# Banded attention and a two-layer MLP on one core: the order table of all five engines replaced by that of another search

## The chip, the core and the metric

The kernel runs on one core of a Trainium2 chip. The metric is the device time of one execution in microseconds (us), the median of the runs given. The core's engines each take their instructions strictly in order: PE (TensorE, matrix products), DVE (VectorE), ACT (ScalarE), POOL (GpSimd) and SP (SyncE, which here only issues DMA transfers). What one engine needs of another it waits for at a semaphore, and everything queued behind the waiting instruction waits too.

## The reference

```python
def _attn_ref(q_l, k_l, v_l, q_g, k_g, v_g):          # 8 batches, 8 heads, 512 local + 32 global, D = 64
    k_all = np.concatenate([k_g, k_l], axis=2); v_all = np.concatenate([v_g, v_l], axis=2)
    out_g = np.matmul(sm(scale * np.matmul(q_g, k_all.transpose(0, 1, 3, 2))), v_all)
    s_ll = np.where(np.abs(pos[:, None] - pos[None, :]) <= 32, scale * q_l @ k_l.T, -1e9)
    s_l = np.concatenate([scale * q_l @ k_g.T, s_ll], axis=-1)
    out_l = np.matmul(sm(s_l), v_all)                 # sm: softmax over the last axis
    return np.concatenate([out_g, out_l], axis=2)
def _moe_ref(x, w_in, w_out):                         # x 4352 x 512, w_in 512 x 2048, w_out 2048 x 512
    h = x @ w_in
    return (h * np.cos(h)) @ w_out
reference = _moe_ref(_attn_ref(...).transpose(0, 2, 1, 3).reshape(B * S, H * D), w_in, w_out)
```

## The kernel before

All products run in fp16 planes: a value is split into a high and a low part, and a product is three PE products (high by high, high by low, low by high). Batch 0 and the scores of batch 1 run in fp32 while the weights are still being decoded.

**Attention** goes by pairs of heads (`b, p`: batch and pair). Of a pair, `load_qk` fetches q and k, `qk_a` to `qk_c` find a scale (`qk_b` is one small PE product, `pm_qk`), `qk_d` splits: ACT writes the high part `qa` (line 916), DVE the low part `kl` (line 917). `qk_e` moves halves of them between partitions by three SP steps, the first from `qa` (lines 928, 929), the second from `kl` once the first has landed (line 931), the third after the second (line 933). Then `sc_a` makes the scores of one of four windows on PE (`ps`, lines 1184 and 1185, the first against `kh`, the second against `kl`), `sc_b` adds the mask on DVE, `sc_c` takes the exponential on ACT, `sc_d` normalizes on POOL (line 1230), casts to the high plane on ACT (line 1235) and subtracts for the low plane on POOL (line 1237), both planes in `plx`. `sc_e` transposes a window's planes by one SP transfer into `ptb` (line 1242), and `av_a` multiplies them with v on PE (`acc`, line 1274). Of a batch, `v_q`, `v_b` and `v_c` find v's scale (`v_b` is the PE product `pm_v`, line 855).

**The MLP** goes by chunks of 256 tokens, 17 of them (the last holds the global rows), each in eight blocks of 256 hidden columns: `m1_a` (24 products `ph` on PE, line 1432), `m1_b` to `m1_d` (cosine and product on ACT and DVE, split into `gh` on ACT, line 1478, and `gl` on POOL, line 1479), `m2_a` (products `po`, lines 1585 to 1587). From chunk 4 on, the first two blocks of a chunk take seven smaller products in place of eight (`sv_a`, `sv_y`, line 1530). PE interleaves the MLP of one batch with the attention of the next.

**The weights** (`w_in_load`, `w_in_max`, `w_in_piece`, and the same for `w_out`) are loaded as 64-bit integers, searched for their maximum and decoded on DVE, ACT and POOL during the first part of the program.

What sets the order: `body` records every step's instructions, and then reads `ORDER`, one string per engine. A word such as `23.4x3` names step 23, its instruction 4 of that engine, and three in a row; each instruction named gets a dependency on the one named before it, so that the string is the engine's queue:

```python
        for name, line in ORDER.items():
            mine = [[i for i in step if i.engine == getattr(E_, name)] for step in steps]
            at_, prev, used = defaultdict(int), None, set()
            for word in line.split():
                word, _, times = word.partition("x")
                k, _, i = word.partition(".")
                at_[k] = int(i or at_[k])
                for _ in range(int(times or 1)):
                    ins = mine[int(k)][at_[k]]
                    at_[k] += 1
                    if prev is not None:
                        tc.add_manual_dep(ins, prev.name, order, reason="order")
                    prev = ins
```

On ACT the exponential and the cosine need different function tables; a table load (`ACT_TABLE_LOAD`) is put in wherever the order changes from the one to the other.

Of the kernel before, what the change touches and what calls it, by code (L numbers as in the profile page):

```python
# [22 lines left out]
        18x4 22x4 23.4 23.0 23.5 23.1x2 23.6 23.3 23.7 27x4 29.4x3 29.0 29.7 29.1x3 33 33.2 33.1 33.3 35  # L23
        35.4 35.1x3 35.5x3 28x8 34x8 40 40.4 40.1 40.5 40.2 40.6x2 40.3 57 49 69x4 39x8 41x8 74 74.2
        74.1 74.3 64x24 67x24 72x24 108 108.2 108.1 108.3 91x24 106x24 125x24 109 109.4 109.1 109.5
        109.2 109.6 109.3 109.7 135x24 110x2 110.4 110.2 110.5x2 110.3 110.7 124 112x8 113x8 127 127.2
        127.1 127.3 141 141.4x4 141.1x3 143x24 149x8 150 150.4 150.1 150.5 150.2 150.6 150.3 150.7 164x3
        155x5 151x8 152x8 156x20 157x8 164 189x5 164x19 189x3 170x3 170.4 170.3 164 176x22 171x2 189x4
        176x2 187x2 171x18 195x4 196 196.2 196.1 196.3 187x22 206x24 208.6 208.0 208.7 208.1x2 208.8x2
        208.3 208.10 208.4 208.11 208.5 204 209x4 210 210.2 210.1 210.3 227x24 229x2 229.6x2 229.2 229.8  # L30
        229.3x3 229.9x3 250 250.6x3 250.1x2 250.9x2 250.3x3 250.11 274 274.6 274.1x3 274.7x2 274.4 274.9
        274.5 274.10x2 288.6 288.0 288.7 288.1x3 288.8x4 288.4x2 230x18 231x3 231.4x4 231.3 233 233.2
        233.1 233.3 300x2 300.6x3 300.2x2 300.9 300.4x2 300.10 248x24 272x21 234 234.2 234.1 234.3
        230x18 300 303.6 303.0x3 303.7x3 303.3x3 303.10x2 251x2 252x4 272x3 311x12 251x2 253x4 251x32
        313.6 313.0x5 313.7x3 313.5 313.10x2 318x2 318.6x2 318.2x4 318.8x4 286x24 275x13 276x8 325
        325.6x2 325.1 325.8x3 325.2x3 325.11 325.5 329.6 329.0 329.7 275x23 289 290 349x4 329.1x5
        329.8x4 294x60 333x2 333.6x2 333.2x4 333.8x4 289x35 349x5 371x5 307x30 319 322 307x30 381x5
        349x15 371x19 326 330 339.6 339.0x3 339.7x2 339.3 339.9x2 326x3 330x3 339.4x2 339.11 335x4 340x4
        351x3 351.6 351.3x3 351.7x5 381x19 356x4 357x8 358 395x24 373x4 374x8 410x24 384x4 397x5 424x24
        436x2 436.6x2 436.2x4 436.8x4 398x4 453.6 453.0x3 453.7x4 453.3x2 453.11 453.5 397x31 412x4 413  # L40
        468 468.6 468.1x3 468.7x3 468.4 468.10x2 468.5 427x4 434x24 451x24 438x4 484.6 484.0x2 484.7
        484.2x3 484.8 439 466x22 454x4 466x2 455x4 482x24 484x2 484.5 484.11 499.6x2 499.0x4 499.8x2
        499.4 470x4 471x8 454x32 485x4 497x17 486x8 492x60 499.10x2 499.5 515x24 497x7 532x24 500x4 501
        517.6x2 517.0 517.8 517.1x3 517.9 517.4 517.10x2 517.5 534 534.6x2 534.1x2 534.8 534.3 534.9
# [12 lines left out]
        806.0x3 806.7 806.3 806.8x2 806.4x2 806.10x2 851x4 864x17 826x7 826.9x2 826.7x2 826.11 852x8
        856x60 827x7 827.9 827.7x2 827.10x2 878x6 868x4 878x18 846x3 848x3 894x24 881x36 882x4 909x24
        847x3 849x3 897 858x3 859x3 866x10 897x3 898 866x2 880 880.6 880.1 880.7x2 880.2x3 880.9x3 880.5
        896.6x5 896.0x4 896.11 896.4x2 912x4 917x12 932x13 911x4 911.6x6 911.4x2 917x4 921x4 919.6 919.0  # L60
        932x3 919x2 919.7x3 917x8 919x2 919.3x3 934 934.6 934.1x3 934.7 934.4x2 934.8x4 932x8 939x36
        940x4 955x8 955.9x3 953x24 955.8 973x24 956.3x3 956.0x3 956.9x2 956.6x2 956.11 956.8 960x4 961x8
        993x24 962 1007x24 980x4 975x3 977x3 976x3 978 1024x24 981x8 985x60 997x4 978x2 987x3 988x3
        995x4 995.6x6 995.4x2 1009.6x2 1009.0x2 1009.8 1010x36 1011x4 1009x3 1009.2x4 1041x23 1027 1041
        1026x2 1026.6x6 1026.2x4 1028x4 1029 1049x24 1044x3 1043x2 1043.6 1043.2 1043.7x5 1043.3x3 1051
        1051.6 1044 1051.1 1051.7x5 1051.2x4 1064x24 1066.6x4 1066.0x2 1066.10x2 1066.2x4 1053x4 1070x36
        1071x4 1084x24 1086x2 1086.3x6 1086.2 1086.9x2 1104x24 1086 1087.3x5 1087.0x3 1087.8x4 1124x24
        1091 1092x8 1106x3 1138x6 1091x3 1093 1138x18 1111x4 1108x3 1112x8 1116x60 1154x14 1128x4 1118x3
# [1846 lines left out]
```

## Time and profile before

| | before |
|---|---|
| time, median of 3 runs | 927.91 us (926.1 to 930.22) |
| the profiled execution: its time, its span | 926.53 us, 924.7 us |
| PE busy | 876.5 us (95% of the span), 8126 products |
| ACT busy | 707.6 us (77%) |
| DVE busy | 633.4 us (68%) |
| POOL busy | 511.3 us (55%) |
| granted PE clock, mean over the span | 0.986 |

PE's share of 95% is a mean over parts of the program that differ. The stretches of the span, with each engine's busy time in each, tell which engine a part hangs on; the list of PE's waits tells what the rest of its time was spent on. A wait is the time in which PE had nothing running; short ones are partly hidden, since products overlap at their ends.

### The profile page before, as it was taken

To read this page: it belongs to the slowest core of one execution; us is meant where nothing else is said; L and a number is where in the kernel's file an instruction comes from. 1 tells how busy PE (TensorE), PEld (TensorE's weight loads), DVE (VectorE), ACT (ScalarE), POOL (GpSimd) and SP (SyncE) were. 2 spreads that over 40 slices of the span, in tenths; PEclk is the share of its full clock that TensorE was granted. 3 is DMA by queue.
4 is the path that set the end of the run, shared out by engine and by line. 5 is a ranking of instruction groups with operands and counts; after the bars stand their busy time and mean duration, and the time that the engine had idled before them with its cause. 6 is when DMAs were issued, how large, how long until landed. Compare 5 with 4: busy or idle time off the path is not lost.

```text
span 924.7 us, 21457 instructions
## 1 busy us (share of the span) xinstructions
PE 876.5 (95%) x8126; PEld 634.2 (69%) x8126; DVE 633.4 (68%) x1684; ACT 707.6 (77%) x1400; POOL 511.3 (55%) x765
## 2 busy tenths in 40 slices
PE   4879888999979999999999999999999999999997
PEld 3668645576756786767777776768686868686853
DVE  6998857599877887787679666778766645451520
ACT  5789998789969889888789798978888856453440
POOL 2577799736727656646565455565655554320340
PEclk9799999999999999999999999999999999999999
DMA  9774516876467666464566654573532524000000
GB/s 359 279 272 162 167 24 148 163 197 153 93 142 146 140 146 113 114 162 92 101 138 157 137 102 102 130 185 77 133 69 51 110 47 84 1 24 1 24 24 23
DMA packets 162423, 110.80 MB, mean 120 GB/s; under 512 B 140176, under 2 KB 142608, under 8 KB 160400
## 3 DMA queue, kind: packets, MB, share of 16 engines
q1 hardware_dynamic: 162176, 109.31, 48.6%
q8 instruction: 63, 1.03, 0.5%
q14 instruction: 40, 0.33, 0.1%
q10 hardware_dynamic: 144, 0.13, 0.1%
HBM read 51.61 MB, written 8.91 MB: 65 GB/s over the span
## 4 chain that ended last, share of the span: by engine, by line
PE 56%; ACT 11%; DVE 11%; POOL 11%; DMA 5%; issue 4%; SPq 1%; DVEq 0%; POOLq 0%; ACTq 0%
PE ph L1432 23%; PE po L1587 7%; PE po L1585 7%; PE po L1586 7%; PE po L1530 4%; DMA ptb<-plx 3%; ACT t L774 2%; PE acc L1274 2%; ACT L774 2%; POOL t L1230 2%; POOL gl L1479 2%; POOL plx L1237 2%; DVE kl L917 1%; POOL plx L819 1%; ACT u L774 1%
## 5 line engine op out<-in xcount | busy, mean ns | idle before, releaser
L1432 PE MATMUL ph<-xh,wi_h 128*128 128x256 f16 x1024 | 280.2, 274 | 4.4 <-DVE gf L1467 4.3
L1432 PE MATMUL ph<-xl,wi_h 128*128 128x256 f16 x1024 | 280.2, 274 | 2.1 <-DVE xl L1110 2.1
L1432 PE MATMUL ph<-xh,wi_l 128*128 128x256 f16 x1024 | 279.4, 274 | 0.2 <-POOL wi_l L516 0.2
L1432 PEld LDWEIGHTS <-wi_h 128*128 128x128 f16 x2176 | 211.5, 98 | 40.0 <-DVE gf L1467 5.1
L1479 POOL TENSOR_TENSOR gl<-gf,gh 128x512 f16<-128x512 f32 x136 | 158.8, 1179 | 129.2 <-ACT gh L1478 113.0
L1586 PE MATMUL po<-wo_l,gh 128*128 128x512 f16 x440 | 161.9, 380 | 0.0
L1585 PE MATMUL po<-wo_h,gh 128*128 128x512 f16 x440 | 157.3, 381 | 0.7 <-DVE o L1605 0.7
L1587 PE MATMUL po<-wo_h,gl 128*128 128x512 f16 x440 | 157.9, 381 | 0.0
L1450 DVE SCALAR_TENSOR_TENSOR u<-ph,ca,u 128x512 f32<-128x512 f32 x136 | 100.5, 743 | 67.5 <-ACT u L1449 67.2
L1230 POOL TENSOR_SCALAR t<-t,sm 128x224 f32<-128x224 f32 (+1 forms) x192 | 83.8, 452 | 111.9 <-DVE sm L1221 64.6
L1449 ACT ACTIVATE u<-ph,quarter,ca 128x512 int32<-128x512 f32 x136 | 104.0, 770 | 54.4 <-PE ph L1432 36.5
L1467 DVE SCALAR_TENSOR_TENSOR gf<-u,ph 128x512 f32<-128x512 f32 x136 | 91.8, 682 | 77.7 <-ACT u L774 57.6
L774 ACT ACTIVATE t<-t,mn 128x224 f32<-128x224 f32 (+1 forms) x256 | 118.2, 463 | 19.7 <-DVE mn L1025 11.6
L1237 POOL TENSOR_TENSOR plx<-t,plx 128x192 f16<-128x192 f32 (+1 forms) x192 | 113.0, 612 | 32.8 <-ACT plx L1235 19.9
L774 ACT ACTIVATE u<-u,halfpi 128x512 f32<-128x512 f32 x136 | 95.9, 718 | 31.7 <-DVE u L1450 30.9
L1432 PEld LDWEIGHTS <-wi_l 128*128 128x128 f16 x1088 | 106.9, 98 | 17.3 <-issue 2.9
L774 ACT ACT_TABLE_LOAD x77 | 98.8, 1283 | 1.2
L1201 DVE CUSTOM_DVE_ANT_0 t<-ps,msk,al 128x192 f32<-128x192 f32 (+1 forms) x192 | 77.5, 426 | 27.9 <-PE ps L1185 27.4
L1478 ACT CAST gh<-gf 128x512 f16<-128x512 f32 x136 | 81.3, 609 | 16.2 <-DVE gf L1467 9.4
L1587 PEld LDWEIGHTS <-gl 128*128 128x128 f16 x440 | 43.1, 98 | 51.2 <-issue 0.7
L1586 PEld LDWEIGHTS <-gh 128*128 128x128 f16 x440 | 43.1, 98 | 46.8 <-issue 1.7
L1585 PEld LDWEIGHTS <-gh 128*128 128x128 f16 x440 | 42.8, 98 | 42.6 <-issue 1.5
(281 smaller groups left out, 1528.4 us busy)
## 6 DMA issues: line engine op xcount, KB each, us to landing
qkr<-qk SPq DMA_DIRECT2D x24, 608.0 KB, 4.7
vr<-v SPq DMA_DIRECT2D x8, 1280.0 KB, 6.0
out<-o SPq DMA_DIRECT2D x33, 256.0 KB, 2.8
kh<-qa SPq DMA_DIRECT2D x48, 152.0 KB, 2.8
wo_h<-wo SPq DMA_DIRECT2D x8, 512.0 KB, 4.5
wo_l<-wo SPq DMA_DIRECT2D x8, 512.0 KB, 3.6
qa<-kl SPq DMA_DIRECT2D x24, 152.0 KB, 2.7
kl<-kl SPq DMA_DIRECT2D x24, 152.0 KB, 2.4
```

Source lines behind the costliest of these rows:

```text
L774: ins = nc.scalar.activation(*a, **k).ins
L1230: nc.gpsimd.tensor_scalar(t[:, h], t[:, h], r[:, h : h + 1], 1.0, op0=ALU.mult, op1=ALU.mult)
L1237: nc.gpsimd.tensor_tensor(lo[:, h], t[:, h], hi[:, h], op=ALU.subtract)
L1432: nc.tensor.matmul((ph.rearrange("p a (k t) -> p a k t", k=2)[:, :, a] if seven(c, j) else ph[:, a]), w[:, kc, f], x[:, kc, q], start=firs ...
L1449: nc.scalar.activation(u.bitcast(I32), ph, AF.Identity, bias=quarter, scale=a)
L1450: nc.vector.scalar_tensor_tensor(u, ph, a, u.bitcast(I32), op0=ALU.mult, op1=ALU.subtract)
L1467: nc.vector.scalar_tensor_tensor(gf, w, 0.25 if c >= CW else 0.5, st.pop(("ph", c, j)).rearrange("p a b -> p (a b)"), op0=ALU.mult, op1=AL ...
L1478: nc.scalar.copy(gh, gf)
L1479: nc.gpsimd.tensor_tensor(gl, gf, gh, op=ALU.subtract)
L1585: nc.tensor.matmul(po[k], gh[:, q], wo_h[:, f], start=(f == first), stop=False, skip_group_check=c >= CW)
L1586: nc.tensor.matmul(po[k], gh[:, q], wo_l[:, f], start=False, stop=False, skip_group_check=c >= CW)
L1587: nc.tensor.matmul(po[k], gl[:, q], wo_h[:, f], start=False, stop=(f == NJ - 1), skip_group_check=c >= CW)
```

## The change

Only the table `ORDER` is new: the same steps, the same instructions, the same tiles and buffers, in another order on every engine. The table comes from a search like that of before, in which twice the time was reserved behind each transpose. It names 7862 instructions of PE, 1046 of ACT, 1390 of DVE, 758 of POOL and 346 of SP, each once, as before; they stand on average 21 places from where they stood on PE, 3.8 on ACT, 6.3 on DVE, 4.2 on POOL and 2.0 on SP. The table is four lines longer, so that every line number of the code behind it grows by 4. One row of each of two strings:

```diff
     "PE": """
-        18x4 22x4 23.4 23.0 23.5 23.1x2 23.6 23.3 23.7 27x4 29.4x3 29.0 29.7 29.1x3 33 33.2 33.1 33.3 35
+        18x4 22x4 23.4 23.0 23.5 23.1x3 23.6x2 27x4 29x3 29.4x3 29.3 29.7 33 33.2 33.1 33.3 28x8 35 35.4
...
     "Activation": """
-        20x4 25x4 44 23.1 23.0 44 31x4 47 48x2 29.1 48x2 47 37x4 29.0 53 35.1 35.0 40.1 53 40.0 56 66 59
+        20x4 25x4 44x2 31x3 37 31 47 29.1 23.1 23.0 47 37x3 48x4 29.0 53 35x2 40.1 40.0 53 56 66 59 56
```

Since ACT's order changes more often between exponential and cosine, its program now holds 88 table loads in place of 78.

The rows below are those of the built programs. First POOL's queue around batch 2, pair 2 (`t_2_0` to `t_2_2` are that pair's score tiles, the window's number or buffer behind; `plx` on the left is a low plane, written after ACT's cast of the same tile) and blocks 5 to 7 of chunk 2 and 0, 1 of chunk 3 (`gl_5` to `gl_7`, `gl_0`, `gl_1`). Before:

```order
L1479 TENSOR_TENSOR gl_5_3005<-gf_5_3006,gh_5_3004 128x512
L1237 TENSOR_TENSOR plx<-t_2_0_2913,plx 128x192
L1479 TENSOR_TENSOR gl_6_3086<-gf_6_3087,gh_6_3085 128x512
L1237 TENSOR_TENSOR plx<-t_2_1_2988,plx 128x224
L1237 TENSOR_TENSOR plx<-t_2_0_2913,plx 128x192
L1237 TENSOR_TENSOR plx<-t_2_2_3074,plx 128x224
L1513 TENSOR_TENSOR twwfo<-ws_1_0_2752,twwfo 128x256
L1237 TENSOR_TENSOR plx<-t_2_2_3074,plx 128x192
L1479 TENSOR_TENSOR gl_7_3190<-gf_7_3191,gh_7_3189 128x512
L1237 TENSOR_TENSOR plx<-t_2_2_3074,plx 128x192
L1479 TENSOR_TENSOR gl_0_3288<-gf_0_3289,gh_0_3287 128x512
L1479 TENSOR_TENSOR gl_1_3432<-gf_1_3433,gh_1_3431 128x512
```

POOL at the same place in the changed program:

```order
L1483 TENSOR_TENSOR gl_6_3086<-gf_6_3087,gh_6_3085 128x512
L1241 TENSOR_TENSOR plx<-t_2_1_2988,plx 128x224
L1241 TENSOR_TENSOR plx<-t_2_0_2913,plx 128x192 x2
L1241 TENSOR_TENSOR plx<-t_2_1_2988,plx 128x224
L1483 TENSOR_TENSOR gl_5_3005<-gf_5_3006,gh_5_3004 128x512
L1241 TENSOR_TENSOR plx<-t_2_2_3074,plx 128x192
L1483 TENSOR_TENSOR gl_7_3190<-gf_7_3191,gh_7_3189 128x512
L1241 TENSOR_TENSOR plx<-t_2_2_3074,plx 128x224 x2
```

The low planes of `t_2_1` and `t_2_0` now stand together behind `gl_6`, and `gl_0` and `gl_1` have moved behind this piece.

ACT's queue at that place, where `qa_0_3078` is the high part of batch 3, pair 0. Before:

```order
L1235 CAST plx<-t_2_2_3074 128x2x224
L1478 CAST gh_6_3085<-gf_6_3087 128x512
L1235 CAST plx<-t_2_0_2913 128x2x192
L1235 CAST plx<-t_2_2_3074 128x2x192
L1293 ACTIVATE xh_2844<-acc_1_3131,xs 128x512
L916 ACTIVATE qa_0_3078<-qkr_0_2944,qs_0_3067 128x1216
L1478 CAST gh_7_3189<-gf_7_3191 128x512
L1478 CAST gh_0_3287<-gf_0_3289 128x512
```

ACT at the same place in the changed program:

```order
L1482 CAST gh_5_3004<-gf_5_3006 128x512
L1453 ACTIVATE u_1_3318<-ph_1_3293,quarter,ca_2517 128x512
L778 ACTIVATE t_3_0_3251,sm_3_3625<-t_3_0_3251,mn_3_0_3252 128x192 x2
L1239 CAST plx<-t_2_2_3074 128x2x192
L920 ACTIVATE qa_0_3078<-qkr_0_2944,qs_0_3067 128x1216
L1239 CAST plx<-t_2_0_2913 128x2x192
L778 ACTIVATE gt_1_3255,gsm_1_3634<-gt_1_3255,gmn_1_3256 128x544
L1239 CAST plx<-t_2_1_2988 128x2x224
```

The casts of `t_2_0` and `t_2_1` stood ahead of `qa_0` and now stand behind it.

SP's queue around the three moves of batch 3, pair 0 (`kh_0_3082`, `qa_0_3078`, `kl_0_3079`) and the four transposes of batch 2, pair 2 (`ptb<-plx` behind them). Before:

```order
L929 DMA kh_0_3082<-qa_0_3078 64x1216
L928 DMA kh_0_3082<-qa_0_3078 64x1216
L931 DMA qa_0_3078<-kl_0_3079 64x1216
L1242 DMA_TRANSPOSE ptb<-plx 128x8x128
L792 DMA qkr_2_3722<-qk 128x1216
L1242 DMA_TRANSPOSE ptb<-plx 128x8x128 x2
L933 DMA kl_0_3079<-kl_0_3079 64x1216
L1242 DMA_TRANSPOSE ptb<-plx 128x8x128
```

SP at the same place in the changed program:

```order
L933 DMA kh_0_3082<-qa_0_3078 64x1216
L932 DMA kh_0_3082<-qa_0_3078 64x1216
L935 DMA qa_0_3078<-kl_0_3079 64x1216
L1246 DMA_TRANSPOSE ptb<-plx 128x8x128
L937 DMA kl_0_3079<-kl_0_3079 64x1216
L1246 DMA_TRANSPOSE ptb<-plx 128x8x128 x3
L796 DMA qkr_2_3722<-qk 128x1216
```

The third move, `kl_0` to itself, stood behind three transposes and a load and now stands behind one transpose.

SP's first transfers of the program, before (`qkr_0`, `qf_1` and `kf_1` are q and k of pairs 0 and 1, `wo_h<-wi` and `plx<-wi` pieces of the raw first weights, held in rooms that are free at that time):

```order
L836 DMA qkr_0_118<-qkf 128x352 x2
L642 DMA wo_h<-wi 128x1024
L1683 DMA msk<-mask 128x896
L836 DMA qf_1_122<-qkf 128x352
L836 DMA kf_1_123<-qkf 128x352
L642 DMA plx<-wi 128x1024
```

SP's first transfers in the changed program:

```order
L840 DMA qkr_0_118<-qkf 128x352 x2
L840 DMA qf_1_122<-qkf 128x352
L840 DMA kf_1_123<-qkf 128x352
L1687 DMA msk<-mask 128x896
L646 DMA wo_h<-wi 128x1024
L646 DMA plx<-wi 128x1024
```

The first piece of weights has moved behind q and k of pair 1 and the mask.

## Rows read from the trace of the kernel before

**Rows 1.** Stretches: start and end, length, busy time (instructions) by engine, clock, DMA, GB/s.

```profile
core 0: us, PE busy (x) PEld busy (x) DVE busy (x) ACT busy (x) POOL busy (x), PEclk, DMA share, GB/s
0.00:10.00 10.00, 1.87 (x8) 1.28 (x8) 2.09 (x12) 1.79 (x3) 1.80 (x7) 1.00 0.81 284
10.00:75.00 65.00, 51.81 (x366) 42.17 (x366) 62.17 (x172) 52.49 (x105) 38.96 (x62) 0.87 0.80 299
75.00:110.00 35.00, 31.51 (x352) 24.32 (x352) 28.86 (x82) 33.68 (x68) 25.91 (x35) 1.00 0.54 182
110.00:183.00 73.00, 65.85 (x514) 38.85 (x513) 46.35 (x136) 61.78 (x140) 67.97 (x111) 0.95 0.46 102
183.00:250.00 67.00, 66.13 (x724) 47.72 (x719) 62.15 (x172) 61.99 (x123) 37.52 (x62) 1.00 0.69 158
250.00:270.00 20.00, 14.94 (x136) 10.42 (x135) 15.86 (x31) 12.82 (x26) 6.08 (x7) 1.00 0.50 100
270.00:750.00 480.00, 476.74 (x4749) 352.32 (x4748) 355.07 (x975) 408.47 (x811) 281.58 (x428) 1.00 0.56 121
750.00:925.00 175.00, 167.69 (x1299) 117.14 (x1297) 60.82 (x113) 74.62 (x129) 51.50 (x56) 1.00 0.10 24
```

**Rows 2.** PE's waits from 188 us to the end: total us, times, longest.

```profile
PE ps L1185 <- DMA kl<-kl: 2.8, 1, 2.8
PE pm_v L855 <- DVE vm L486: 2.3, 1, 2.3
PE acc L1274 <- DMA ptb<-plx: 2.0, 5, 0.6
PE po L1530 <- DVE o L1595: 1.2, 3, 0.8
PE po L1530 <- ACT o L1558: 0.6, 1, 0.6
```

**Rows 3.** DVE in order of time, 248 to 258 us: start, duration, what.

```profile
249.01 0.73 DVE L1294 SCALAR_TENSOR_TENSOR xl<-acc,xs,xh 128x512 f16<-128x512 f32 x1
249.67 6.54 DVE L917 SCALAR_TENSOR_TENSOR kl<-qkr,qs,qa 128x1216 f16<-128x1216 f32 x1
256.13 0.14 DVE L486 TENSOR_SCALAR vm<-vm 128x1 uint32<-128x1 uint32 x1
```

**Rows 4.** All instructions of line 917: shortest, median and longest in ns.

```profile
L917 DVE SCALAR_TENSOR_TENSOR kl<-qkr,qs,qa x24: 1466/1480/6543, 185.1 to 725.1; 128x1216 f16<-128x1216 f32 x24
```

**Rows 5.** POOL in order of time, 243 to 263 us.

```profile
249.90 0.67 POOL L1513 TENSOR_TENSOR twwfo<-ws,twwfo 128x256 f16<-128x256 f32 x1
250.53 0.55 POOL L1237 TENSOR_TENSOR plx<-t,plx 128x192 f16<-128x192 f32 x1
251.04 1.16 POOL L1479 TENSOR_TENSOR gl<-gf,gh 128x512 f16<-128x512 f32 x1
252.16 0.55 POOL L1237 TENSOR_TENSOR plx<-t,plx 128x192 f16<-128x192 f32 x1
252.66 2.26 POOL L1479 TENSOR_TENSOR gl<-gf,gh 128x512 f16<-128x512 f32 x2
261.70 1.16 POOL L1479 TENSOR_TENSOR gl<-gf,gh 128x512 f16<-128x512 f32 x1 [6.77 <-ACT gh L1478]
```

**Rows 6.** PE in order of time, 252 to 270 us.

```profile
256.33 0.23 PE L855 MATMUL pm_v<-ident,vm 128*128 128x128 bf16 x1 [2.27 <-DVE vm L486]
...
261.36 0.27 PE L1432 MATMUL ph<-xh,wi_h 128*128 128x256 f16 x1
261.47 0.27 PE L1432 MATMUL ph<-xl,wi_h 128*128 128x256 f16 x1
...
266.37 0.24 PE L1185 MATMUL ps<-kl,qa 128*128 128x192 f16 x1 [2.79 <-DMA kl<-kl]
```

**Rows 7.** SP's issues in order of time, 244 to 268 us.

```profile
256.28 0.46 SPq L931 DMA_DIRECT2D qa<-kl  x1
256.85 1.93 SPq L1242 DMA_TRANSPOSE ptb<-plx  x1
258.83 0.58 SPq L792 DMA_DIRECT2D qkr<-qk  x1
259.51 3.90 SPq L1242 DMA_TRANSPOSE ptb<-plx  x2
263.46 0.58 SPq L933 DMA_DIRECT2D kl<-kl  x1
```

**Rows 8.** From the page's list of DMA issues: count, KB each, median us to landing.

```profile
qa<-kl SPq DMA_DIRECT2D x24, 152.0 KB, 2.7
```

**Rows 9.** DVE in order of time, 0 to 12 us.

```profile
2.40 0.23 DVE L438 TENSOR_SCALAR ident<-ident 128x128 bf16<-128x128 f32 x1 [1.22 <-POOL ident masks.py:199]
8.48 0.74 DVE L561 TENSOR_SCALAR lo_wi<-wo_h 128x1024 uint16<-128x1024 uint16 x1 [5.85 <-DMA wo_h<-wi]
9.20 0.45 DVE L1025 CUSTOM_DVE_ANT_0 t<-fps,msk,alf 128x224 f32<-128x224 f32 x1
```

**Rows 10.** ACT's groups: line, operation, count, then busy us, mean ns, idle before.

```profile
L774 ACT ACT_TABLE_LOAD x77 | 98.8, 1283 | 1.2
```

**Rows 11.** ACT in order of time, 242 to 256 us.

```profile
247.28 1.12 ACT L1478 CAST gh<-gf 128x512 f16<-128x512 f32 x2
248.43 1.28 ACT L774 ACT_TABLE_LOAD   x1
249.72 0.46 ACT L774 ACTIVATE t<-t,mn 128x192 f32<-128x192 f32 x1
```

More of the change, by code (lines that the diff above doesn't have):

```diff
@@ L28 @@
[L28 to L32, printed above, removed]
@@ new lines @@
+        695.10x2 695.8 713x7 696x7 696.9x3 696.7x2 700x4 701x8 702 733x24 715x3 717x2 720x4 721x8 725x60
+        737x4 747x24 764x8 716x3 781x11 717 781x5 764x16 750x36 751x4 718x3 767 781x2 727x3 728x3 735x4
+        735.6x3 735.4 735.9x3 735.5 749 749.6 749.1 749.7x4 749.2 749.11 749.3x3 768x4 769 766.6x2
+        766.0x2 766.8x3 766.2x4 766.11 781x3 783 781x3 784x4 789x24 804x24 783.6x4 783.1x3 783.10
+        783.4x2 783.11 824x24 793x4 810x36 811x4 844x24 831x4 791.6x2 791.0x2 791.8x4 791.2x4 806.6
@@ new lines @@
+        1156x2 1156.2x4 1171 1171.6 1171.1x2 1171.7x2 1171.3x3 1171.9x3 1181x4 1169 1192x8 1177x21 1179
+        1179.6x5 1179.1 1179.11 1179.2x4 1194 1194.6x3 1194.1x3 1194.9x2 1194.4x2 1194.11 1213x24
+        1199x36 1200x4 1233x24 1215x2 1215.3x3 1215.2 1215.9x3 1215.6x3 1216.3x2 1216.0 1216.5x2
+        1216.1x2 1216.9x3 1216.7x2 1220x4 1221x8 1222 1253x24 1240x4 1235x3 1237x3 1241x8 1245x60
+        1267x24 1284x6 1257x4 1236x3 1247x2 1284x18 1247 1270x36 1271x4 1248x3 1238x3 1255x3 1255.6x3
@@ new lines @@
+        1493x24 1459x36 1460x4 1475x7 1475.9x3 1475.7x2 1476.3x2 1476.0x3 1476.5x2 1476.9x3 1476.7x2
+        1513x24 1480x4 1481x8 1482 1495x3 1497x2 1527x24 1544x24 1500x4 1501x8 1505x60 1496x3 1561x8
+        1517x4 1498x2 1497 1561x16 1507x3 1508x3 1498 1569x15 1515x3 1515.6x6 1515.3x3 1530x36 1531x4
+        1547 1584x24 1529.6x2 1529.0x2 1529.8x2 1529.2x4 1529.10x2 1548x2 1549 1548x2 1569x9 1564x4
+        1546.6x4 1573x4 1546 1546.0 1546.11 1546.1x5 1563.6 1563.0x5 1563.7x2 1563.5 1563.9x3 1571x4
@@ new lines @@
+        1676.1x5 1676.11 1677x4 1691x2 1691.6x3 1678 1691x2 1691.2x2 1691.11 1691.4x2 1692x4 1701x4
+        1699x2 1699.6x2 1699.2 1699.8x4 1699.3x3 1713.6x4 1713.0x5 1713.10x2 1713.5 1711x24 1730x14
+        1717x10 1718x4 1730x10 1732x8 1732.9 1732.8 1732.10x2 1747x24 1733x3 1733.9x2 1733.3 1733.11
+        1733.4x4 1767x24 1778x24 1749x3 1751x3 1737x4 1733 1792x24 1761x3 1802x15 1750x3 1738x8 1762x3
+        1754x4 1755x8 1717x26 1759x60 1807x17 1770x4 1752x3 1769x2 1769.6x3 1769.2x4 1769.9x3 1802x9
@@ new lines @@
+        1780.6x2 1780.0 1780.8x2 1780.1x5 1780.10x2 1794x3 1794.6 1794.3x3 1794.7x5 1781x36 1782x4
+        1804.6x6 1804.0x6 1809.6x3 1809.0x6 1809.9x3 1807x7 1819x5 1819.6x6 1819.5 1817x24 1831x3
+        1831.9x2 1831.3x6 1831.11 1829x24 1832x6 1832.9x3 1838x13 1840x3 1838x11 1842x3 1853x2 1823x36
+        1845x60 1853x22 1847x3 1832.6x3 1858x24 1863x24 1841x3 1868x24 1873x24 1843x3 1878x24 1848x3
+        1855x4 1855.6x4 1855.4x2 1855.10x2 1860x5 1860.6x4 1860.5 1860.10x2 1865.6 1865.0x2 1865.7
@@ new lines @@
+        1865.2x2 1865.8x4 1865.4x2 1888x10 1870x2 1870.6x5 1870.2x4 1870.11 1897x22 1888x14 1875.6
+        1897x2 1875.0 1875.7x4 1875.1x5 1875.11 1880.6x2 1880.0x3 1880.8x4 1880.3x3 1910x24 1915x24
+        1890x6 1890.9x3 1890.6x3 1891.3 1891.0x3 1891.4x8 1920x24 1899x3 1901x3 1925x24 1900x3 1904x3
+        1905x3 1930x14 1902x3 1935x24 1912.6 1912.0x2 1912.7x5 1912.2x4 1917x12 1930x10 1922 1922.6x6
+        1922.1x5 1927x2 1927.6x2 1927.2 1927.8x4 1927.3x3 1945x24 1954x24 1932.6x4 1932.0x4 1932.10x2
@@ new lines @@
+        1603 1623 1620.2 1618x2 1657 1643 1657 1681 1684 1683.1 1681x2 1684 1673x2 1681 1682.1 1684
+        1682.0 1682.2 1684 1683.0 1742.1 1685 1741x2 1742.0 1744.1 1682 1743.1 1744.0 1710 1729 1746
+        1683.2 1743.0 1683 1742.2x2 1741 1688 1696 1741 1777 1744.3 1743.3 1766 1744.2 1743.2 1777
+        1796.1 1795 1796.0 1795 1797.1 1791 1796.2 1797.0 1798x2 1796 1798.3 1795 1798.2 1797.3 1801
+        1795 1797.2 1799 1791 1816 1828 1837 1806 1852 1857.1 1862.1 1857.0 1862.0 1867 1877 1887 1896
@@ L272 @@
+        1872 1909 1914x2 1919.1 1934 1944 1919.0 1953 1924 1966 1929 1971x2 1976.1 1991 1976.0 1981 1986
+        2001 2010 2022
     """,
     "SP": """
[L274 to L277 removed]
@@ L286 @@
[L286 to L289 removed]
+        0.1 0.0 2x2 1 3 5 4x2 8 6x2 7 10 9 12 11 13.1 13.0 16 78 16 14 15x2 17 14 79 77 17 81 84 80 82
@@ L290 @@
+        1446 1469 1524 1521 1518 1516x2 1519 1520 1523 1541 1581 1574 1576 1577 1575 1572.1 1572.0 1580
+        1599 1578 1601 1600 1655 1651 1649 1647 1650 1652 1647 1654 1671 1700.1 1702 1700.0 1726 1708
+        1725 1703 1727 1705 1706 1704 1774 1773 1771 1772 1825 1811 1813 1812 1826 1810 1814 1885 1884
+        1941 1942 1998 1999 2030 2038
     """,
```

439 lines of the change are left out of this document (202 added, 237 removed), and 32 rows, old and new, of the table ORDER.

## The prediction

> **What bounds the kernel now.** Read the stretches first [rows 1]. After 270 us PE is busy for 476.74 of 480 us and then 167.69 of 175 us, of which the last few are the program's end; no order can gain much there, since the products themselves are unchanged. Ahead of 183 us PE is not the bound. DVE is busy 62.17 of 65 us up to 75 us, then ACT 33.68 of 35 us, then POOL 67.97 of 73 us: a relay in which the weights are decoded and batch 1 is prepared. PE's idle time there (13.2, 3.5 and 7.2 us in these three stretches, their length less PE's busy time) is filled by whichever engine carries the relay, so a wait of PE that goes there comes back as another one. What is left is 183 to 750 us, and there one stretch stands out: 250 to 270 us, PE busy 14.94 of 20.
>
> PE's waits from 188 us on say the same [rows 2]: 2.8 us once for `kl`, 2.3 us once for `pm_v`, and 2.0 us in five pieces for transposes, the thing that the search was told to leave more room for. The first two have one cause. At 249.67 us DVE begins `kl` of batch 3, pair 0 and is through 6.54 us later [rows 3], where the median of the 24 is 1.48 us [rows 4]. POOL shows why: it runs one instruction after another until 252.66 + 2.26 = 254.92 us [rows 5], and `kl` ends at 256.21 us, 1.29 us after that. DVE made its pass when POOL paused. Behind `kl` on DVE stood the last step ahead of `pm_v`, which PE then gets 2.27 us late [rows 6], and on SP the second move of the pair, issued at 256.28 us, with a transpose, a load, two more transposes and only then, at 263.46 us, the third move [rows 7], for which PE waits 2.79 us at 266.37 us [rows 6].
>
> The Trainium skill ("SBUF — State Buffer", Who interferes with whom) says that a DVE instruction with two inputs in SBUF and a GpSimd instruction share a pair of ports, and that whichever starts first holds it for its whole instruction. By that rule `kl` would lose at most the one POOL instruction in progress, 1.16 us at the longest; the trace disagrees, as it lost 5.06 us to a run of them.
>
> **The change, part by part.**
>
> (a) *The starved `kl`.* In the new order ACT casts `t_2_0` and `t_2_1` after `qa_0`, and POOL's queue stands at the low planes of just these two. POOL must therefore pause until at least one cast after `qa_0`, and `kl`, which needs `qa_0` alone, meets a free POOL. So I take 6.54 - 1.48 = 5.06 us off DVE. On SP the third move now stands behind one transpose. Its second move lands 2.7 us after its issue [rows 8], about 259.0 us in the old clock, so the third move no longer waits from 259.0 to 263.46 us: another 4.5 us at most. Against this, PE asks earlier: between `pm_qk` and the first product with `kl` of this pair stood 138 products of 256 columns and stand 96, 42 x 0.11 = 4.6 us less (0.11 us is the distance of two starts [rows 6]); the other kinds differ by 0.1 us. Together `kl` comes 5.1 + 4.5 = 9.6 us earlier and is asked for 4.6 us earlier, against a wait of 2.8 us: no wait is left, with some 2 us to spare. `pm_v` is asked for 2.6 us of PE work earlier, but its last DVE step now stands ahead of `kl`, not behind it. Gain: 2.3 + 2.8 = 5.1 us; what is late next is the transposes of batch 2, pair 2, which stand on SP behind the second move, so I give back 0.8 us. Term: **-4.3 us**, with ends 0 and -5.1.
>
> (b) *Transposes after 188 us.* All five waits gone would be -2.0 us [rows 2]; as many again would be +2.0. The order alone does not show doubled room: counted with the spacing of PE's products, the work between a window's scores and the first product that reads its transposed plane grows by 0.9 us on average over the 96 windows of batches 2 to 7. Where the least room is under 1 us that is enough for most, so **-1.5 us**.
>
> (c) *The beginning.* DVE idles 5.85 us until the first weights land at 8.48 us, and the first masking step follows at 9.20 us [rows 9]. In the new order the mask and pair 1 come ahead of the megabyte of weights, so the four masking steps of pair 0 (distance 0.4 us, 1.5 us together) can run in that gap, and perhaps the four of pair 1 (3.0 us in all). DVE carries the relay to 75 us, so what it gains goes on to ACT and POOL, as far as the later weights are there. I take **-1.5 us**, ends -3.0 and +1.5 (weights landing later by the 352 + 224 KB put ahead of them, at the first stretch's 284 GB/s 2.0 us, less the half that DVE can cover). Behind this, POOL's amount of work up to the end of batch 1's planes is the same, and so is what PE has done by then, within 0.5 us.
>
> (d) *Ten more table loads.* Each is 1283 ns [rows 10]: 12.8 us more of ACT. From 183 to 750 us ACT is idle for 67 - 61.99 + 20 - 12.82 + 480 - 408.47 = 83.7 us [rows 1], which covers them, and two of the ten fall between batch 1's exponentials and the first ones of batch 2, where ACT is idle 11.2 of 73 us. Taken at **0**; if that cover fails for the two, +2.6 us. The skill ("ScalarE: Activation LUTs", What ACT_TABLE_LOAD costs) counts 2.66 us for a switch, with a drain behind the load; by it the ten would be 26.6 us. The trace shows the next exponential at 249.72 us, right after a load that began at 248.43 and took 1.28 [rows 11], so no drain.
>
> (e) *New waits.* Nearly every engine's order is new, and the waits of [rows 2] are what one such order leaves. A new one like `kl` costs up to 5.1 us; one of the 24 in the trace was hit so [rows 4]. **+1.0 us**, ends 0 and +5.1.
>
> Sum: -4.3 - 1.5 - 1.5 + 0 + 1.0 = -6.3 us against the profiled execution's 926.5 us: 920.2 us. The median of the runs lies 1.4 us above that execution; I put the new median at **921 us**, 0.7% faster.
>
> **The rivals.** *No change* (about 925 us): the waits move. For it: PE's idle time ahead of 183 us belongs to the relay, the gain of (a) is one accident of timing, and the next order has its own; with (c) at zero and a new wait of 4 us the sum is -1.8 us. If the skill's rule on the ports held, (a) could recover only 1.2 us, and the rest would be a wait that stays: 926.5 - 1.2 - 1.5 - 1.5 + 1.0 = 923.3 us. Against it: the free POOL at `kl` follows from the queues, not from timing.
>
> *Slower* (about 934 us): ACT becomes the engine that PE follows. It has the thinnest cover from 75 us on: 33.68 of 35 us, and 61.99 of 67 us in 183 to 250 us [rows 1]. If the ten loads fall where exponentials are already waited for, all 12.8 us show, less the 5.8 us of (a) and (b): 926.5 + 7.0 = 933.5 us. It decides from some 6 exposed loads (7.4 us) on. For it: the stretch 183 to 250 us has only 5.0 us of idle ACT. Against it: PE waits for ACT directly 0.6 us after 188 us [rows 2], and 480 us follow in which ACT idles 15%.
>
> *The change does not do what it says*: room behind transposes stays as it is, and (b) is 0 or +2. That alone gives 922 to 924 us, inside the range.
>
> **How the numbers follow.** A measurement of this kernel tells about 0.5% (4.6 us) from no change. Forecast with its near variants (913 to 923 us): 0.52. No change, waits moved (923.3 to 932.5 us): 0.31. Slower by the table loads or a chain of new waits: 0.17. The range goes from the sum with both good ends, -5.1 - 2.0 - 3.0 with no new wait, 916.4 us, and 2 us for the gap between executions, to the middle of the slower case: 914 to 932 us.
>
> **What would show it.** In the changed profile: line 921's longest duration near 1.5 to 2.5 us; no PE wait over 1 us for `kl<-kl` or `pm_v`; waits for `ptb<-plx` after 188 us at 0.5 us or less; DVE's first masking step at 5 to 6.5 us; `pm_v` of batch 3 on PE within a us of its neighbours; 88 loads on ACT and its busy time near 720 us with PE still over 99% busy from 270 to 750 us. The prediction is wrong if another DVE instruction of this kind is starved where PE follows it, if the POOL stretch ends later than 183 us, or if PE's waits for ACT after 183 us exceed some 5 us.

## The result

Over seven executions each, the changed kernel took **919.67 us** (median; 917.73 to 923.7) and the kernel before 927.91 us (926.1 to 930.8): a ratio of **0.9917**, interval 0.9893 to 0.9942. The forecast was 921 us. A second measurement gave 921.19 against 926.77 us, 0.9941 (0.992 to 0.9962). So the gain was measured twice, at 8.2 and at 5.6 us.

The two profiled executions differ by less, 923.7 against 926.53 us. The changed kernel's is the slowest of its seven, the other lies under its median. Their difference must therefore not be read as the gain; what is read from them is where each loses time.

By stretch, the changed kernel's trace answers to [rows 1] as follows (start and end, length, busy time of each engine with its instructions, clock, share of the DMA engines, GB/s):

```profile
10.00:75.00 65.00, 50.07 (x359) 40.80 (x360) 58.99 (x165) 50.30 (x100) 38.35 (x61) 0.84 0.79 296
183.00:250.00 67.00, 65.98 (x746) 47.82 (x745) 61.66 (x177) 61.32 (x126) 37.88 (x61) 1.00 0.69 161
250.00:270.00 20.00, 19.96 (x170) 13.73 (x169) 14.98 (x39) 18.50 (x37) 12.08 (x18) 1.00 0.77 155
270.00:750.00 480.00, 476.16 (x4741) 351.50 (x4740) 355.53 (x967) 412.14 (x814) 282.00 (x424) 1.00 0.56 119
```

The stretch that stood out does so no more: from 250 to 270 us PE (the first pair of numbers) is busy 19.96 us in place of 14.94. From 270 to 750 us nothing moved, 476.16 against 476.74 us. In the first long stretch PE is busy 1.7 us less and DVE 3.2 us; up to 10 us PE was busy 1.9 us more (3.72 against 1.87). So the beginning did not get better by this trace.

PE's waits from 188 us on, against [rows 2] (what it waited for: us in total, times, longest; the six costliest and one more):

```profile
PE po L1534 <- ACT o L1562: 0.9, 2, 0.6
PE ph L1436 <- DVE qs L864: 0.5, 1, 0.5
PE ps L1188 <- DVE r L894: 0.5, 1, 0.5
PE po L1589 <- ACT o L1562: 0.5, 1, 0.5
PE gacc L1369 <- DVE mn L1205: 0.5, 1, 0.5
PE acc L1278 <- DMA ptb<-plx: 0.5, 1, 0.5
...
PE ps L1189 <- DMA kl<-kl: 0.2, 1, 0.2
```

The waits of 2.8 us for `kl` and 2.3 us for `pm_v` are gone, those for transposes (`ptb<-plx`) fell from 2.0 to 0.5 us, and nothing of more than 0.6 us took their place.

`kl` of batch 3, pair 0 on DVE (start, duration), against [rows 3 to 5]:

```profile
249.57 1.47 DVE L921 SCALAR_TENSOR_TENSOR kl<-qkr,qs,qa 128x1216 f16<-128x1216 f32 x1
```

All 24 (count, then shortest, median and longest in ns):

```profile
L921 DVE SCALAR_TENSOR_TENSOR kl<-qkr,qs,qa x24: 1465/1479/2109, 187.6 to 715.5; 128x1216 f16<-128x1216 f32 x24
```

POOL there:

```profile
248.40 1.17 POOL L1483 TENSOR_TENSOR gl<-gf,gh 128x512 f16<-128x512 f32 x1
249.80 3.29 POOL L1241 TENSOR_TENSOR plx<-t,plx 128x224 f16<-128x224 f32 x4 [0.23 <-ACT plx L1239]
```

POOL paused for 0.23 us, waiting for ACT's cast, just as DVE came to `kl`. That was enough: `kl` took 1.47 us in place of 6.54. The longest of the 24 is now 2.11 us.

ACT's table loads, all but the program's first, against [rows 10]:

```profile
L778 ACT ACT_TABLE_LOAD x87 | 111.6, 1283 | 1.4
```

And DVE's waits in the first 14 us, against [rows 9] (us in total, times, longest):

```profile
DVE t L1029 <- DMA msk<-mask: 4.2, 1, 4.2
DVE lo_wi L565 <- DMA wo_h<-wi: 2.9, 1, 2.9
```

Ten loads more, as counted. And DVE still idles 7.1 us in the first 12, now first for the mask and then for the weights.

### The profile page after: what moved, and what is told of

Read it like the earlier page. It is cut to its first block, busy times and chain, and to the rows that moved or that the text cites. A ratio compares the mean times of both kernels' runs of the same rounds, so it can differ in the third digit from the quotient of the medians.

```text
span 921.9 us, 21466 instructions
## 1 busy us (share of the span) xinstructions
PE 879.9 (95%) x8126; PEld 636.0 (69%) x8126; DVE 632.8 (69%) x1684; ACT 718.0 (78%) x1410; POOL 514.5 (56%) x765
## 5 line engine op out<-in xcount | busy, mean ns | idle before, releaser
L778 ACT ACTIVATE t<-t,mn 128x224 f32<-128x224 f32 (+1 forms) x256 | 118.1, 463 | 19.9 <-DVE mn L1029 12.0
```

Of the source, the lines that this page charges most:

```text
L778: ins = nc.scalar.activation(*a, **k).ins
```

## The experiments

All compare with the kernel before on the same chip. Where a table of orders was put together anew, the line numbers of the program are some 30 smaller than in the kernel before; the names are the same.

### Where in the program the gain lies

Two mixtures of the two tables. Up to 187 us both programs have done the same work, save for some ten instructions, so the queues can be cut there. In the queue of each engine:

```diff
 h_late
-before, to its end
+before up to 187 us; then the new order, without what has been done
 h_early
-before, to its end
+the new order up to 187 us; then that of before, without what has been done
```

> The order of before for everything that starts up to 187 us there, the new order for all that follows. Theory (the gain is the starved kl of batch 3, pair 0, and the transposes after 188 us): PE's losses after 200 us fall from 19 to 14 us, 5.4 us faster than before, about 922.5 us, and the profile shows no instruction of line 917's kind above 2.5 us. Rival (the gain lies in the first 187 us, since the median moved by 8 us and the two profiled executions by 3 only): no more than 2 us faster, about 926 us or above.

> The new order for everything that starts up to 187 us there, the order of before for all that follows. Theory: the beginning is worth 1.5 to 3 us, 925 to 926.5 us; the starved kl near 250 us is back at 6.5 us and PE waits 2.3 us for pm_v and 2.8 us for kl again. Rival (the beginning holds most of the gain): 5 us or more faster, 923 us or below. Third reading, from the two profiled executions alone, where the changed kernel's first 200 us lost 3 us more: 931 us.

> The changed kernel as it is, for a second profiled execution. Theory: 8 us faster than before as measured, about 919.7 us; PE's losses after 200 us as in the first profile (14 us), those before 200 us some 3 to 4 us smaller than in the first profile, which was the slowest of its seven executions. Rival: the first profile is typical of the beginning, and its losses of 53 us come again.

`h_late` took 920.32 us against 926.77 us of before, **0.9935** (0.9915 to 0.9955); `h_early` 928.49 us, **1.0015** (0.9998 to 1.0032); the unchanged new kernel 0.9941, as said. The theory holds for the late part. For the beginning theory, rival and third reading (931 us) all fall: it is worth nothing, or costs up to 3 us. The second profile of the changed kernel came out as expected: its first `kl` (next paragraph) is 2.3 us earlier than in the first profile, and the rest nearly the same.

A look into the traces says the same. The work ahead of batch 2 ends about where the first `kl` of line 917's kind begins. The row that groups the 24 gives that start (the first number after the three durations). In `h_late`:

```profile
L887 DVE SCALAR_TENSOR_TENSOR kl<-qkr,qs,qa x24: 1465/1478/2134, 184.3 to 709.8; 128x1216 f16<-128x1216 f32 x24
```

And in `h_early`:

```profile
L883 DVE SCALAR_TENSOR_TENSOR kl<-qkr,qs,qa x24: 1470/1478/6545, 188.0 to 728.4; 128x1216 f16<-128x1216 f32 x24
```

In `h_early` the 6.5 us of the starved `kl` are back. From this point to the end of the span (span less that start, one profiled execution each):

| program | first `kl` | span | rest |
|---|---|---|---|
| before | 185.1 | 924.7 | 739.6 |
| `h_early` | 188.0 | 926.9 | 738.9 |
| changed | 187.6 | 921.9 | 734.3 |
| changed, second profile | 185.3 | 918.7 | 733.4 |
| `h_late` | 184.3 | 916.2 | 731.9 |
| `pool_pause` (below) | 184.5 | 917.3 | 732.8 |
| `no_pause` (below) | 188.8 | 926.3 | 737.5 |

The new order behind 187 us is worth about 6 us. That figure hardly depends on the beginning: the two further mixtures below have a rest of 738.3 us (`start14`, the order of before) and 732.4 us (`late14`, the new one). The first `kl` itself is no such firm figure. It moves by some 2 us between two profiles of one and the same program (187.6 and 185.3 here; 184.3 and 186.5 for `h_late` and its repeat), so that one profile decides little about the beginning.

### Is it the starved instruction? Two edits, one each way

In the kernel before, two instructions moved so that POOL must wait for a cast of ACT when `kl` comes (words of the table: step and instruction; 477.0 is the cast of window 3, 392.2 a piece of the weight sums, 447.0 `qa`):

```diff
 ACT
-474.0 477.0 457.0 447.0 465.0 481.0 525.0 525.1 526.0 496.0
+474.0 457.0 447.0 465.0 481.0 525.0 525.1 526.0 477.0 496.0
 POOL
-476.3 392.2 477.2 465.0 477.3 481.0
+476.3 477.2 465.0 477.3 392.2 481.0
```

> The kernel before with two instructions moved: ACT's cast of window 3 of batch 2, pair 2 behind three exponentials, and POOL's piece of the weight sums behind that window's low planes, so that POOL has to wait for the cast just when DVE comes to kl of batch 3, pair 0. Theory (kl is kept out by POOL's back-to-back instructions and goes in at the first pause): kl takes 1.5 to 2.5 us in place of 6.5, PE's waits of 2.3 us for pm_v and 2.8 us for kl go, 4.5 to 5 us faster, about 923 us. Rival (kl is slow for another reason, its operands or transfers beside it): kl still takes 6 us or more, and the time stays at 927 to 928 us.

It took 921.77 us, **0.9945** (0.9928 to 0.9962), 5.0 us less than before. DVE in its trace:

```profile
249.05 1.56 DVE L884 SCALAR_TENSOR_TENSOR kl<-qkr,qs,qa 128x1216 f16<-128x1216 f32 x1
```

POOL at the same time (in brackets the idle time before, and what ended it):

```profile
247.65 1.68 POOL L1204 TENSOR_TENSOR plx<-t,plx 128x224 f16<-128x224 f32 x3
250.86 0.55 POOL L1204 TENSOR_TENSOR plx<-t,plx 128x192 f16<-128x192 f32 x1 [1.53 <-ACT plx L1202]
```

And the stretch from 250 to 270 us, columns as above:

```profile
250.00:270.00 20.00, 20.00 (x177) 14.36 (x175) 16.19 (x50) 17.75 (x37) 8.55 (x12) 1.00 0.63 136
```

POOL pauses for 1.53 us, `kl` passes, PE is busy for all 20 us. Two moved words of a table give as much as the new one did on the same chip, within the noise: 0.9945 against 0.9941, and a rest of 732.8 us against 733.4 and 734.3 us. (The first measurement of the new one was 0.9917.)

The other way, in the changed kernel: ACT's cast of window 1 (475.0) ahead of an exponential (529.0), so that POOL need not pause.

```diff
 ACT
-474.0 529.0 475.0 457.0
+474.0 475.0 529.0 457.0
```

> The changed kernel with one instruction moved: ACT's cast of window 1 of batch 2, pair 2 ahead of the exponential of the global rows, so that POOL, which waited 0.23 us for this cast at 249.57 us, need not pause when DVE comes to kl of batch 3, pair 0. Theory (kl goes in only where POOL pauses): kl takes 6 to 8 us again in place of 1.5, its second move is issued near 257 us, PE waits 2 to 4 us for kl, and the time is 3 to 6 us above the changed kernel's, 923 to 926 us. Rival (kl is not kept out by POOL, and the gain came from the rest of the order): kl stays below 2.5 us and the time at the changed kernel's 920 to 921 us.

It took 924.03 us against 928.02 us, 0.9962 (0.9947 to 0.9977), between the changed kernel and before. Its DVE:

```profile
250.86 6.16 DVE L887 SCALAR_TENSOR_TENSOR kl<-qkr,qs,qa 128x1216 f16<-128x1216 f32 x1
```

Its POOL:

```profile
250.82 2.18 POOL L1207 TENSOR_TENSOR plx<-t,plx 128x224 f16<-128x224 f32 x4
252.97 1.15 POOL L1449 TENSOR_TENSOR gl<-gf,gh 128x512 f16<-128x512 f32 x1
254.08 0.54 POOL L1207 TENSOR_TENSOR plx<-t,plx 128x192 f16<-128x192 f32 x1
254.59 1.15 POOL L1449 TENSOR_TENSOR gl<-gf,gh 128x512 f16<-128x512 f32 x1
258.97 1.18 POOL L1207 TENSOR_TENSOR plx<-t,plx 128x224 f16<-128x224 f32 x2 [3.23 <-ACT plx L1205]
```

And PE's only wait from 250 to 275 us:

```profile
PE ps L1154 <- DVE gsm L1310: 2.4, 1, 2.4
```

One swapped pair on ACT starves `kl` again, for 6.16 us, until POOL's run ends at 255.74 us. The theory holds for the instruction, but I had named the wrong victim: PE waits 2.4 us not for `kl` but for scores, whose DVE steps stood behind it. The price is at the low end, 2 to 4 us by the ratios. In this profile, that of the slowest of its twelve executions, PE's granted clock also stood at 0.50, the lower of its two levels, from 260.7 to 264.1 us, about 1 us behind that wait. With `kl` starved the new order is, by the ratio, still 3.5 us (2.1 to 4.9) ahead of before: `pm_v`, whose last DVE step now stands ahead of `kl`, is not waited for, and `kl` itself for 0.6 us only.

### The queue of SP alone

In the kernel before, the third move of that pair (494.0) ahead of a load and two transposes:

```diff
 SP
-505.0 544.0 504.0 507.0 494.0 506.0
+505.0 494.0 544.0 504.0 507.0 506.0
```

> The kernel before with one transfer moved: SP's third move of batch 3, pair 0 directly behind the transpose of window 1, ahead of a load and two transposes. Theory (two separate delays behind one starved instruction): kl still takes 6.5 us and PE still waits 2.3 us for pm_v, but the third move is issued near 259 us and no longer waited for, 2.8 us faster, about 924 us. Rival (PE is late for kl by the starved instruction alone, and the queue does not matter): a wait of 2 us or more for kl stays, and the time too, 926 to 927 us.

It took 927.38 us, 0.9996 (0.9981 to 1.0012): nothing. PE's waits from 250 to 275 us:

```profile
PE pm_v L822 <- DVE vm L453: 2.3, 1, 2.3
PE acc L1241 <- DMA ptb<-plx: 2.1, 2, 1.9
```

SP's issues (start, time on the queue):

```profile
255.25 0.46 SPq L898 DMA_DIRECT2D qa<-kl  x1
255.81 2.49 SPq L1209 DMA_TRANSPOSE ptb<-plx  x1
259.18 0.46 SPq L900 DMA_DIRECT2D kl<-kl  x1
259.69 0.58 SPq L759 DMA_DIRECT2D qkr<-qk  x1
260.38 5.63 SPq L1209 DMA_TRANSPOSE ptb<-plx  x3
```

The wait for `kl` went as expected, and 2.1 us came back as a wait for the transposes now behind it. Mine was wrong, and of the rival only the time was right: with the second move as late as before, the queue behind it was full whatever stood first in it. The late second move is the starved instruction's doing: in `pool_pause`, with SP's order untouched, neither wait appears between 250 and 270 us.

### What ten table loads cost

Three kernels, each the one before with ten more loads. A tiny exponential between two cosines forces two:

```diff
 m1_c, for five pairs (chunk, block)
             table_act("Sin", w, w, AF.Sin, scale=TWOPI, bias=halfpi)
+            if (c, j) in (...):
+                nc.scalar.activation(warm, alf, AF.Exp)
```

> The kernel before with five exponentials of one element per partition put between cosines of chunks 2 and 3 (200 to 245 us), each of which forces two more table loads: ten loads, 12.8 us, and 5 tiny instructions more on ACT where it was idle 5.0 of 67 us. Rival of the prediction (ACT becomes the engine that PE follows): PE waits for ACT or for what hangs on it, 5 to 8 us slower, 932 to 935 us. Theory of the prediction, taken to its end (PE runs far enough behind ACT for even this): less than 2 us slower. Between the two I expect 4 us, since only 5 us are free there.

> The same ten loads and five tiny exponentials, put between cosines of chunks 4 to 7 (308 to 455 us), where ACT was busy 85% of the time. Theory (ten more loads cost nothing where ACT has its 15% of idle time): within 1 us of before, about 927 us, with ACT's busy time 13 us up. Rival (each load is waited for): 12 us slower, 939 us.

`loads_thin` took 934.9 us, 1.0083 (1.0063 to 1.0103), 6.9 us slower: inside the rival's 5 to 8 us, and not my 4. In its shifted timing the longest `kl` was 2.385 us; by `pool_pause` that alone gives 5 us back, so I estimate the loads at some 12 us.

That `kl` was not starved here qualifies what the two edits above seemed to say. Batch 3, pair 0, on DVE and then on POOL:

```profile
263.66 1.57 DVE L884 SCALAR_TENSOR_TENSOR kl<-qkr,qs,qa 128x1216 f16<-128x1216 f32 x1
262.26 1.69 POOL L1204 TENSOR_TENSOR plx<-t,plx 128x224 f16<-128x224 f32 x3
263.90 1.85 POOL L1482 TENSOR_TENSOR twwfo<-ws,twwfo 128x256 f16<-128x256 f32 x1
```

POOL's queue is that of before, and POOL did not pause. Yet `kl` went in between the third `plx` and `twwfo`, and `twwfo` took 1.85 us in place of 0.67 [rows 5]. So a pause was enough to let `kl` in, but it is not needed every time.

`loads_wide` took 940.52 us, **1.0145** (1.0122 to 1.0167): 12.5 us slower for 12.8 us of loads. The theory has fallen. ACT at one of the five places:

```profile
372.18 1.28 ACT L741 ACT_TABLE_LOAD   x1
373.48 0.72 ACT L741 ACTIVATE u<-u,halfpi 128x512 f32<-128x512 f32 x1
374.22 1.28 ACT L1426 ACT_TABLE_LOAD   x1
375.51 0.20 ACT L1426 ACTIVATE warm<-alf 128x1 f32<-128x1 f32 x1
375.73 1.28 ACT L741 ACT_TABLE_LOAD   x1
377.03 0.72 ACT L741 ACTIVATE u<-u,halfpi 128x512 f32<-128x512 f32 x1
```

PE's costliest waits of that kernel behind 184 us:

```profile
PE acc L1241 <- DMA ptb<-plx: 6.4, 7, 1.6
PE ps L1152 <- DMA kl<-kl: 3.2, 1, 3.2
PE pm_qk L822 <- DVE xg L1343: 2.4, 1, 2.4
PE pm_qk L822 <- DVE xl L1261: 2.3, 1, 2.3
PE pm_v L822 <- DVE vm L453: 2.3, 1, 2.3
```

ACT works without a pause around the pair, so all that stands behind it comes 2.8 us later, and two engines on, PE waits for transposes and DVE; by name it waits for ACT no longer than before, 0.6 us. The waits for `kl` and `pm_v` were there before, too.

That the price equals the ten loads is in part chance. All of PE's waits listed behind 184 us sum to 19.9 us, against 10.5 us before: 9.4 us more. The rest goes with PE's clock (columns as above):

```profile
384.20:387.60 3.40, 3.40 (x10) 1.20 (x11) 3.19 (x11) 2.63 (x6) 3.40 (x9) 0.50 0.00 0
469.50:472.90 3.40, 3.26 (x16) 2.35 (x17) 2.97 (x12) 1.91 (x4) 1.85 (x3) 0.50 0.00 0
```

Right behind the two waits for `pm_qk` the granted clock stood at 0.50 for 3.4 us each, where before it was 1.00 from 270 to 750 us [rows 1]. In the second stretch two products of 256 columns start 0.21 us apart in place of 0.11, so I estimate 1.7 us lost each time, some 3 us in all.

Third, the same number of loads in pauses of ACT:

```diff
 body, behind five steps whose ACT instruction a pause follows
                 f(*a)
+                for fn in {...}.get(len(steps), ()):
+                    nc.scalar.activation(warm, alf, getattr(AF, fn))
```

> The kernel before with ten more table loads again, but in five pauses of ACT of 2.73, 3.11, 3.89, 2.72 and 2.03 us (at 311.5, 439.4, 667.1, 689.5 and 710.6 us): in each two tiny exponentials or cosines of one element per partition, the second of which brings the table back, so that two loads and both instructions (2.96 us) fall into the pause. Theory formed on loads_wide (a load costs its time where ACT has no pause right behind it, whatever its share of idle time; in a pause it costs nothing): 1.4 us stand out of the five pauses, 0.5 to 2 us slower, about 929 us. Rival (a switch of tables costs its time wherever it stands): 12.5 us slower as in loads_wide, 940 us.

It took 927.75 us against 927.25, **1.0011** (0.9991 to 1.003): ten loads for half a microsecond, nothing within the noise, and the theory formed on `loads_wide` holds. One of the five pauses:

```profile
437.45 1.28 ACT L1802 ACT_TABLE_LOAD   x1
438.74 0.20 ACT L1802 ACTIVATE warm<-alf 128x1 f32<-128x1 f32 x1
438.96 1.28 ACT L1802 ACT_TABLE_LOAD   x1
440.26 0.20 ACT L1802 ACTIVATE warm<-alf 128x1 f32<-128x1 f32 x1
440.54 0.78 ACT L1416 ACTIVATE u<-ph,quarter,ca 128x512 int32<-128x512 f32 x1
```

The next instruction starts 0.08 us behind the last of the four, so this pause was just filled. The price of a load depends on its place.

### The beginning, and a candidate ahead of both

The same kind of mixture with the cut at 14 us:

```diff
 start14
-before, to its end
+the new order up to 14 us; then that of before
 late14
-the new order, to its end
+before up to 14 us; then the new order
```

> The new order for what starts in the first 14 us there, the order of before for all that follows. Theory (the later arrival of the first weights is what makes the new beginning slower, the rest of the beginning is even): batch 2's first kl starts 1 to 2.5 us later than the 184 to 185 us of before, and the time is 1.5 us above before's, about 929 us. Rival (the new beginning is slowed by its order from 14 to 80 us): first kl and time as before.

> The order of before for what starts in the first 14 us there, the new order for all that follows: the candidate for a version ahead of both. Theory: DVE begins on the weights at 8.5 us again, batch 2's first kl starts at 184 to 185 us, and the time is 1 to 2 us below the changed kernel's, 0.991 to 0.993 of before's. Rival (the beginning is slowed from 14 to 80 us): first kl at 186 us or later and 0.994 of before's or more.

`start14` took 930.03 us, 1.0031 (1.0015 to 1.0048), 2.8 us slower, with the first `kl` at 187.7 us; `late14` 923.44 us, 0.9963 (0.9949 to 0.9978), with the first `kl` at 188.0 us, not at 184 to 185. So the new first 14 us are enough to make the kernel before slower, but the old ones in front of the new order don't make it faster. The two halves don't add; that each order fits only its own opening is a guess. Only DVE's first 14 and SP's first 15 words of the table differ, between `start14` and before as between `late14` and the changed kernel; those of PE, ACT and POOL are the same. Which of DVE's steps or SP's transfers carries the loss stays open.

The old beginning as a whole with the new order from 187 us is the best of the mixtures, and ran a second time:

> The order of before up to 187 us and the new order from there, a second time, as the candidate for a version ahead of both. Theory (the two parts add: the beginning of before, which brings batch 2's first kl to 183 to 186 us, and the new order's 732 to 734 us behind it): 6 to 8 us faster than before, 0.991 to 0.994 of it, first kl at 183 to 186 us. Rival (the first result was luck, and the beginning is worth nothing): the changed kernel's own 0.994 or above, first kl at 186 us or later.

919.66 us against 926.3 us, **0.9924** (0.9904 to 0.9944); its profiled execution, the slowest of its six, had the first `kl` at 186.5 us, outside what the theory wanted. With 0.9935 and 0.9924 it stands beside the changed kernel's 0.9917 and 0.9941: ahead of before, not shown to be ahead of the changed kernel.

## Why the prediction was right, step by step

**The bound.** Right: between 183 and 750 us, 250 to 270 us was the one stretch that the new order mended, by 5.0 us of PE's time (19.96 less 14.94).

**(a) The starved `kl`, -4.3 us.** Right, mechanism and size: -5.0 us by `pool_pause`. Of its two parts as I put them, the DVE time was the cause; the move ahead on SP's queue, which I credited with 4.5 us of room, is worth nothing alone (`third_move`). That POOL must pause followed from the queues, as said, but the pause was 0.23 us long, less than the argument made it sound. And timing had a part in it after all: `loads_thin` has POOL's queue of before and no pause, and `kl` was not starved. The rival *no change*, which called it an accident of timing, had a point. The Trainium skill ("SBUF — State Buffer", Who interferes with whom) says that issue order decides who blocks. The trace agrees: in the changed kernel `kl` went first, and POOL's four `plx` took 3.29 us against 2.18 us for the same four in `no_pause`. In `loads_thin` `kl` lost only the rest of the one POOL instruction in progress; in the kernel before and in `no_pause` it lost a run of them. What makes the difference no run shows.

**(b) Transposes, -1.5 us.** Their waits fell by 1.5 us in the trace, but no gain in time is shown for it: with the order of before and only the pause, the rest behind the first `kl` is 732.8 us, no more than with the new order, although 1.5 us of waits for transposes are left. Either what the transposes gave went into small waits for ACT and DVE, or the 2.0 us of before were not typical: `h_early`, with the order of before behind 187 us, shows 0.7 us. That doubled room made this kernel faster is therefore not shown.

**(c) The beginning, -1.5 us.** Wrong, there is no gain: between 0 and +3 us by `h_early`, +2.8 us (1.4 to 4.5) for the first 14 us alone. The masking steps did come earlier, at 6.84 us in place of 9.20, after a wait for the mask of 4.2 us, though not at the 5 to 6.5 us named. The weights came to DVE at 11.30 us in place of 8.48, and that side of the sum, which I had put at +1.5 us for the end of the range, was at least as large. One of the prediction's own signs of being wrong came true here: POOL's busy stretch ahead of batch 2 ended at 187.6 us (185.4 in the second profile) in place of 182.5, later than the 183 us named.

**(d) Ten table loads, 0.** Right number, wrong reason. I took the share of idle time as cover, and `loads_wide`, where ACT has that very share, was 12.5 us slower, some 9 us by PE's waits and some 3 us by the clock that fell behind two of them. They cost nothing where a pause stands right behind them (`loads_idle`). That the changed order has its ten in such places, or has made room for them by the end of the stall, is inferred from its time and from PE's small waits; it was not shown load by load. The rival *slower* was thus nearer than its 0.17 made it: its price for ten badly placed loads was about right, and the choice of places alone decided against it. The Trainium skill's 2.66 us for a switch ("ScalarE: Activation LUTs", What ACT_TABLE_LOAD costs) would have made `loads_wide` 26.6 us slower by the prediction's reckoning. The trace disagrees: a load takes 1.28 us, and the next instruction begins 0.02 us behind it (372.18 + 1.28 against 373.48 us), with no drain.

**(e) New waits, +1.0 us.** None above 0.6 us behind 188 us. The allowance covered the beginning's loss by luck.

So the sum, -6.3 us, lay between the two measurements, -8.2 and -5.6 us, with one term a little small, two gains that are not there or not shown, an allowance that was not used, and one zero whose reason fell. The terms as measured give -5 us, or less with the beginning's loss; what makes up the difference to -5.6 and -8.2 us stays open. That the sum came so close is partly luck. (It also gives 920.2 + 1.4 = 921.6 us, not quite the 921 put down.)

## What to carry to other kernels

When one instruction of a kind takes four times its median, look at which other engine works without a pause until just before it ends, and give that engine a pause there: two moved words of the order were worth as much as a new search on the same chip. An engine's share of idle time was no cover for added work; the pause right behind the place was. And moving a late transfer up a full queue handed the wait to what it passed.

## What the runs showed of the hardware

A DVE instruction with two operands in SBUF (`kl`) got almost nothing done here while POOL's instructions kept it out. In four programs it ended the same time behind the POOL instruction after which it went in: before, 256.21 against 254.92 us, 1.29 us; `no_pause`, 257.02 against 255.74 us, 1.28 us; `pool_pause`, 250.61 against 249.33 us, 1.28 us; `loads_thin`, 265.23 against 263.95 us, 1.28 us. That is the whole instruction (1.48 us) but for 0.2 us, whether it had stood for 0.3 or 5 us.

A pause of POOL of 0.23 us let it in. Without a pause it was passed over six times in a row, in the kernel before at 249.67 us and in `no_pause` at 250.86 us. Elsewhere it went in between two POOL instructions without a pause: in the kernel before at 293.84, 409.48, 512.87 and 661.00 us (the first took 2.40 us and held up the `plx` behind it), and in `loads_thin`. What decides which of the two happens is open.

After PE's waits of 2.3 and 2.4 us in `loads_wide` its granted clock stood at 0.50 for 3.4 us each; after the waits of 2.3 and 2.8 us in the kernel before it stayed at 1.00.
